# A's fifth row block of x^T phi(k) as seven half-size products of 64 columns, ahead of KV

## The chip, the core and the metric

One core of a Trainium2 chip runs the whole kernel in one launch. The metric is the device time of the execution in microseconds, median of three runs. Every run of the kernel is compared with the kernel before on the same chip. TensorE is called PE (its weight loads PEld), VectorE DVE, ScalarE ACT, GpSimd POOL, SyncE SP.

## The reference

Two blocks of linear attention, A and B, read the same x (1 x 2048 x 640, bf16) with weights of their own, and a gate mixes their outputs row by row.

```python
def _A_ref(x, wqkv, wo):
    B, S, D = x.shape
    H = 32; Dh = D // H
    qkv = (lambda x, *d: x.transpose(*d))((x @ wqkv).reshape(B, S, 3, H, Dh), 2, 0, 3, 1, 4)
    q, k, v = qkv[0], qkv[1], qkv[2]
    phi = lambda t: jnp.where(t > 0, t + 1, jnp.exp(t)) + 1e-6
    pq, pk = phi(q), phi(k)
    kv = jnp.einsum("bhsd,bhse->bhde", pk, v)
    z = jnp.einsum("bhsd->bhd", pk)
    num = jnp.einsum("bhqd,bhde->bhqe", pq, kv)
    den = jnp.einsum("bhqd,bhd->bhq", pq, z)[..., None] + 1e-6
    o = num / den
    return (lambda x, *d: x.transpose(*d))(o, 0, 2, 1, 3).reshape(B, S, D) @ wo
...
g = _sigmoid((x * gate_w).sum(-1, keepdims=True))
return g * a + (1 - g) * b
```

Because v = x Wv, the state of a head is kv = phi(k)^T x Wv. The kernel first forms G = x^T phi(k), a 640 x 640 matrix summed over the 2048 rows of x, then KV = Wv^T G for the 32 diagonal blocks of 20 x 20 (packed six groups wide), then M = KV Wo, and the output is the scaled phi(q) times M.

## The kernel before

x stands in SBUF twice: `xT` with columns on the partitions (five groups of 128, c = 0 to 4), `xn` with rows on them (16 chunks of 128, i = 0 to 15). phi(k) is `pk` (16 chunks of 640 columns), phi(q) transposed is `pqT[b]`. PSUM is used in four slots of two banks; `ps(name, slot)` gives a tile of two banks, `pt[:, 0]` and `pt[:, 1]`, which hold the two halves of 320 columns (HF). Where no slot is named, they take turns.

The stages follow each other on PE: K of A (`k_chunk`), with q of A's first half between, q's second half (`q_pass`), G of A, K of B with A's KV and A's M pushed between the chunks, q of B, G of B, B's KV and M, and the output by pairs of row blocks. From the second K stage on the order of the instructions is the order of the code (`manual_schedule`); the few statements before it, the loads of wv, wo and wk among them, are placed by the scheduler.

G of one block (`g_all`) has two parts. `g_pass` forms row block c = 4 of G, 128 rows, by 16 chunks x 2 halves = 32 matmuls of 320 columns. In its course `z_pass` takes the column sums of phi(k) (`Z`, built by DVE in `z_sum`, `z_half` and `z_last` during q), and DVE turns them into `zsel`. `g_strassen` forms the other 512 rows, seen as a 2 x 2 grid of blocks (256 columns of x, 320 of phi(k), rows of x cut into two halves of 8 chunks), by seven products in the way of Strassen and Winograd, where eight would be needed: 7 x 16 matmuls. The sums of blocks of x are `SX[1]` to `SX[4]` (`x_sum`), those of phi(k) `TK[b][1]` to `TK[b][4]` (`k_sum`); both are DVE adds. The products go into two PSUM tiles, `even` and `odd`, which take turns; p1 (the first product) is copied to SBUF by ACT, u2 and u3 are p1 plus a product, and the results land in `GT[0]` and `GT[1]` (called lo and hi), bf16, one per half of phi(k)'s columns.

Behind the first product stands `rec_pass`: PE forms the denominators for all rows of q from zsel (`by_group`, 40 matmuls on 32 columns of the array each), and `rec(h)` adds the epsilon, multiplies with the gate's factor and takes the reciprocal on DVE, for one half of the rows of q at a time; the result goes to DRAM (`r_store`) and comes back spread over the partitions (`r_load` into `R[h]`). `scale(b, lo, hi, h)` multiplies column groups lo to hi of phi(q), half h, by `R[h]`, on DVE; A's are called between the products of `g_strassen` and after three of B's K chunks.

KV (`kv_mm`) runs over six groups k and, for each, over the five c; a group has two matmuls of 60 or 40 columns on the two halves of the array (`tile_position`). `kv_mask` multiplies with a mask of the diagonal blocks into `KVA`. For A it comes after B's K chunk 1. wv of A is loaded whole (128 x 5 x 640) on SP.

Of the kernel before, what the change touches and what calls it, by code (L numbers as in the profile page):

```python
# [32 lines left out]
def kernel(  # L33
# [273 lines left out]
    def g_pass(b, c, slot):  # L307

        pt = ps(f"g{'AB'[b]}", slot)
        for i in range(ST):  # L310
            if b == 0 and i == 4:
                gate_exp()
            if i == (8 if b else 13):
                zsel = z_pass(b)
                if b:
                    p_diff(part[0])
                else:
                    x_sum(2)
                    gate_done(0)
            if b == 1 and i == 13:  # L320
# [12 lines left out]

    def x_sum(k, cuts=(0, hc)):

        x11, x21 = [xn[:, 0:hc, n:n + ic] for n in (0, ic)]
        x12, x22 = [xn[:, hc:ST, n:n + ic] for n in (0, ic)]
        a, b, op = {
            1: (x21, x22, ALU.subtract), 2: (x11, SX[1], ALU.subtract),
            3: (x21, x11, ALU.subtract), 4: (x12, SX[2], ALU.subtract),  # L340
        }[k]
        for lo, hi in zip(cuts, cuts[1:]):
            add_rows(SX[k][:, lo:hi], a[:, lo:hi], b[:, lo:hi], op)

# [20 lines left out]

    def g_prod(pt, left, right, first, lo=0, hi=hc):

        for i in range(lo, hi):
            for n in range(2):
                nc.tensor.matmul(  # L370
                    pt[:, n, 0:HF], lhsT=left[:, i, n * P:(n + 1) * P], rhs=right[:, i, :],
                    start=(first and i == 0), stop=(i == hc - 1), skip_group_check=not first,
                )

    def g_strassen(b, den):

        x11, x12 = [xn[:, k:k + hc, 0:ic] for k in (0, hc)]
        x22 = xn[:, hc:ST, ic:2 * ic]
# [4 lines left out]
        def temp(name):  # L383
            return work.tile([P, 2, HF], FP32, tag="osb", name=name, bufs=3)

        def add(dst, pt, sb):
            nc.vector.tensor_tensor(out=dst, in0=pt[:, :, 0:HF], in1=sb[:], op=ALU.add)

        even, odd = ps("gs0", 0), ps("gs1", 1)
        g_prod(even, x11, b11, True, 0, 1 - b)  # L390
        rec = den()
        rec(0)
        g_prod(even, x11, b11, True, 1 - b)
        p1 = temp("p1")
        nc.scalar.copy(out=p1[:], in_=even[:, :, 0:HF])
        if b == 0:
            x_sum(3)
        else:
            rec(1)
        g_prod(odd, SX[2], TK[b][2], True)  # L400
        u2 = temp("u2")
        add(u2[:], odd, p1)
        if b == 0:
            x_sum(4)
        else:
            p_diff(part[2])
            p_diff(part[3])
            m_sum(0)
        g_prod(even, x12, b21, False)
        nc.scalar.copy(out=lo[:, 0:2, :], in_=even[:, :, 0:HF])  # L410
        if b == 0:
            rec(1)
        r_load(b, 1, nc.scalar)
        if b == 0:
            wq[1] = load_w(1, "q", nc.scalar)
        scale(b, 0, 2, 0)
        g_prod(odd, SX[3], TK[b][3], False)
        u3 = temp("u3")
        add(u3[:], odd, p1)
        scale(b, 2, 4, 0)  # L420
        even = ps("gs0", 0)
        g_prod(even, SX[1], TK[b][1], True)
        if b == 1:
            load_wo(1, nc.sync)
        add(hi[:, 2:4, :], even, u3)
        scale(*((b, 0, 2, 1) if b else (b, 4, 5, 0)))
        g_prod(odd, x22, TK[b][4], False)
        if b == 1:
            scale(1, 4, 5, 0)
        add(lo[:, 2:4, :], odd, p1)  # L430
        if b == 1:
            scale(1, 2, 4, 1)
        g_prod(even, SX[4], b22, False)
        for n in range(2):
            nc.vector.tensor_tensor(out=hi[:, n, :], in0=even[:, n, 0:HF], in1=u2[:, n], op=ALU.add)
        if b == 0:
            scale(0, 0, 2, 1)
    def z_pass(b):

        dst = ps(f"z{'AB'[b]}", 1 - b)[:, 0, 0:DT * H]  # L440
        for c in range(DT):
            nc.tensor.matmul(
                dst[:, c * H:(c + 1) * H], lhsT=mixed(Z[:, 0], c), rhs=ones[:], start=True, stop=True,
            )
        zsel = work.tile([P, DT, H], BF16, tag="zsel", name="zsel")
        nc.vector.tensor_tensor(
            out=zsel[:], in0=dst.rearrange("p (c h) -> p c h", h=H),
            in1=headE[:, None, :].to_broadcast([P, DT, H]), op=ALU.mult,
        )
        return zsel  # L450
# [16 lines left out]
    def kv_mask(src):  # L467
# [3 lines left out]
        for i, n in ((0, 2), (2, 1)):  # L471
            w = WT[i]
            for r in range(2):
# [4 lines left out]
                )  # L478

    def kv_a():  # L480

        pt = ps("kvA")
        kv_mm(0, pt[:, 0])
        kv_mask(pt[:, 0])

# [30 lines left out]
    def rec_pass(b, zsel, slot):  # L516
# [5 lines left out]
        def rec(h):  # L522
            cols = slice(h * RB, (h + 1) * RB)
            d1 = work.tile([P, RB], FP32, tag="d1", name="d1", bufs=1)
            nc.vector.scalar_tensor_tensor(
                out=d1[:], in0=pt[:, 0, cols], scalar=EPS, in1=ge[b][:, cols], op0=ALU.add, op1=ALU.mult
            )
            rT = work.tile([P, RB], BF16, tag="rT", name="rT")
            with nc.allow_low_precision(reason="a fp32 reciprocal, stored as the bf16 that multiplies bf16"):
                nc.vector.reciprocal(out=rT[:], in_=d1[:])  # L530
            eng = nc.scalar if h else nc.sync
            r_store(b, h, rT, eng)
            if h == 0:
                r_load(b, h, eng)
# [61 lines left out]

    def tmp(name, tag):
        return work.tile([P, HF], FP32, tag=tag, name=name)

    class Pair:  # L600
# [44 lines left out]
        def p6(self):  # L645
            prod(self.at("x"), xT[:, :, 0:SH], TM[1], self.i, True)
            self.u6 = tmp("u6", "ex")
            nc.scalar.copy(out=self.u6[:], in_=self.at("x"))  # L648

        def u25(self):  # L650
            self.v = tmp("v", "zr")
            out_add(self.v[:], self.u6[:], self.p15)

# [22 lines left out]
    def load_w(b, which, eng, cuts=(0, DT)):  # L676
        lo = {"q": 0, "k": D, "v": 2 * D}[which]
        t = wpool.tile([P, DT, D], BF16, tag="w" + which, name=f"w{which}{'AB'[b]}")
# [33 lines left out]

    def g_all(b):

        zsel = g_pass(b, DT - 1, 2 - b)
        g_strassen(b, lambda: rec_pass(b, zsel, 3 - b))

# [4 lines left out]
    for n in range(2):  # L722
        for i in range(CB if n else 0, CB * 2 * n):
            k_chunk(0, i, lifted=i % 2 == 0)
        for m in (0, 2):
# [14 lines left out]
    with tc.manual_schedule():  # L740
        for i in range(hc + 1, ST):
# [26 lines left out]
        q_pass(1, [(m, h) for h in range(2) for m in range(DT)], {0: 2, 2: 3, 4: 4}, (1, 3, 5, 6, 7, 8, 9))  # L768
        g_all(1)
        banks.close()  # L770
# [120 lines left out]
```

## Time and profile before

| | us |
|---|---|
| median of 3 runs (182.39 to 182.6) | 182.46 |
| the profiled execution | 182.69 |
| its span | 180.9 |
| PE busy | 177.1 |
| DVE busy | 147.5 |
| ACT busy | 85.8 |
| POOL busy | 5.4 |

The span runs from the first to the last instruction of the program on the core; the profiled execution's own time lies 1.8 us above it. The clock that PE was granted is 1.0 throughout. Busy time of PE is the time in which at least one matmul is under way, and matmuls overlap, so a full row of PE says that it had no gap, not that it was at its peak. In the timelines a row is a run of equal instructions of one engine: start, length, engine, source line, operation, what it writes and reads, how many, and in brackets the idle time before it with what ended it.

### The profile page before, as it was taken

To read this page: it belongs to the slowest core of one execution; us is meant where nothing else is said; L and a number is where in the kernel's file an instruction comes from. 1 tells how busy PE (TensorE), PEld (TensorE's weight loads), DVE (VectorE), ACT (ScalarE), POOL (GpSimd) and SP (SyncE) were. 2 spreads that over 40 slices of the span, in tenths; PEclk is the share of its full clock that TensorE was granted. 3 is DMA by queue.
4 is the path that set the end of the run, shared out by engine and by line. 5 is a ranking of instruction groups with operands and counts; after the bars stand their busy time and mean duration, and the time that the engine had idled before them with its cause. 6 is when DMAs were issued, how large, how long until landed. Compare 5 with 4: busy or idle time off the path is not lost.

```text
span 180.9 us, 3414 instructions
## 1 busy us (share of the span) xinstructions
PE 177.1 (98%) x1340; PEld 119.3 (66%) x1345; DVE 147.5 (81%) x247; ACT 85.8 (47%) x140; POOL 5.4 (3%) x18
## 2 busy tenths in 40 slices
PE   8999999999999999999999999999999999999993
PEld 4566657765577777777775555677777777677772
DVE  0386868989998896888778999969999799977863
ACT  2245846889971101378784779921101863111010
POOL 6000000000000000000000000000003200000000
PEclk9999999999999999999999999999999999999999
DMA  5999999523100216431116000000325451133323
GB/s 179 209 269 173 244 370 284 112 49 134 58 0 6 70 47 209 110 108 36 57 34 190 19 0 0 0 4 14 125 78 132 137 181 50 36 109 112 109 92 127
DMA packets 22842, 19.33 MB, mean 107 GB/s; under 512 B 10538, under 2 KB 22058, under 8 KB 22826
## 3 DMA queue, kind: packets, MB, share of 16 engines
q1 hardware_dynamic: 20744, 16.95, 34.0%
q10 hardware_dynamic: 2082, 2.17, 3.6%
q8 instruction: 10, 0.16, 0.4%
q14 instruction: 6, 0.05, 0.1%
HBM read 12.29 MB, written 4.53 MB: 93 GB/s over the span
## 4 chain that ended last, share of the span: by engine, by line
PE 97%; issue 0%; DVE 0%
PE gs L370 17%; PE kA L218 12%; PE ox L590 12%; PE kB L218 12%; PE qB L281 12%; PE qA L281 6%; PE oz L590 6%; PE qA L291 5%; PE gB L329 2%; PE gA L329 2%; PE ow L590 2%; PE xt L165 2%; PE qA L301 1%; PE mA L494 1%; PE s L494 1%; PE oy L590 1%
## 5 line engine op out<-in xcount | busy, mean ns | idle before, releaser
L218 PEld LDWEIGHTS <-xT 128*128 128x128 bf16 x320 | 31.0, 98 | 12.8 <-DVE xT L243 0.2
L210 DVE TENSOR_SCALAR e<-e 128x640 bf16<-128x640 bf16 (+2 forms) x53 | 18.9, 357 | 7.3 <-ACT e L205 6.7
L218 PE MATMUL kB<-wkB,xT 128*128 128x320 bf16 x160 | 23.1, 299 | 0.0
L218 PE MATMUL kA<-wkA,xT 128*128 128x320 bf16 (+1 forms) x160 | 22.9, 301 | 0.0
L281 PE MATMUL qB<-xT,wqB 128*128 128x512 bf16 x98 | 21.6, 379 | 0.1
L205 ACT ACTIVATE e<-kB 128x640 bf16<-128x640 f32 x16 | 11.2, 703 | 15.8 <-DMA wqB<-in_B_wqkv_dram 9.4
L281 PEld LDWEIGHTS <-wqB 128*128 128x128 bf16 x100 | 11.7, 117 | 9.7
L205 ACT ACTIVATE e<-kA 128x640 bf16<-128x640 f32 x16 | 11.2, 704 | 8.3 <-PE kA L218 8.3
L205 ACT ACTIVATE e<-qA 128x1024 bf16<-128x1024 f32 (+1 forms) x11 | 10.4, 946 | 6.4 <-PE qA L291 5.1
L648 ACT COPY u<-ox 128x320 f32<-128x320 f32 x8 | 3.4, 425 | 20.6 <-PE ox L590 20.6
L205 ACT ACTIVATE e<-qB 128x1024 bf16<-128x1024 f32 x10 | 10.2, 1023 | 5.6 <-PE qB L281 4.9
L370 PEld LDWEIGHTS <-xn 128*128 128x128 bf16 x96 | 9.2, 98 | 3.9 <-issue 0.4
L370 PEld LDWEIGHTS <-S 128*128 128x128 bf16 x96 | 9.4, 98 | 3.6
L281 PE MATMUL qA<-xT,wqA 128*128 128x512 bf16 x49 | 10.9, 379 | 0.1
L214 DVE SCALAR_TENSOR_TENSOR pk<-kB,e 128x640 bf16<-128x640 f32 x12 | 9.9, 824 | 1.2
L590 PEld LDWEIGHTS <-xT 128*128 128x128 bf16 x85 | 8.1, 98 | 2.9
L590 PEld LDWEIGHTS <-pqTB 128*128 128x128 bf16 x80 | 7.8, 98 | 3.3 <-issue 0.2
L590 PEld LDWEIGHTS <-pqTA 128*128 128x128 bf16 x80 | 7.7, 98 | 2.9
L370 PE MATMUL gs<-pk,xn 128*128 128x320 bf16 x64 | 9.5, 299 | 0.0
L281 PEld LDWEIGHTS <-wqA 128*128 128x128 bf16 x50 | 5.9, 117 | 4.8
L291 PE MATMUL qA<-xT,wqA 128*128 128x512 bf16 x38 | 8.9, 379 | 0.1
L212 DVE TENSOR_TENSOR pk<-pk,e 128x640 bf16<-128x640 bf16 x12 | 5.9, 492 | 2.8 <-ACT pk L209 2.2
(123 smaller groups left out, 296.9 us busy)
## 6 DMA issues: line engine op xcount, KB each, us to landing
xn<-in_A_x_dram SPq DMA_DIRECT2D x1, 2240.0 KB, 10.0
out_dram<-pk SPq DMA_DIRECT2D x14, 160.0 KB, 1.8
wvA<-in_A_wqkv_dram SPq DMA_DIRECT2D x1, 800.0 KB
wkB<-in_B_wqkv_dram SPq DMA_DIRECT2D x1, 800.0 KB, 4.7
wqB<-in_B_wqkv_dram ACTq DMA_DIRECT2D x1, 800.0 KB, 6.5
wvB<-in_B_wqkv_dram SPq DMA_DIRECT2D x1, 800.0 KB
MA<-mA_dram SPq DMA_DIRECT2D x1, 800.0 KB, 6.1
MB<-mB_dram SPq DMA_DIRECT2D x1, 800.0 KB
```

The lines of the kernel that those rows point to most:

```text
L165: nc.tensor.matmul(warm[:, 1, 0:n], lhsT=one_l, rhs=one_r[:, 0:n], start=True, stop=True)
L205: nc.scalar.activation(out=e[:], in_=src, func=ACT.Exp)
L210: nc.vector.tensor_scalar(e[:], e[:], 1.0, EPS, op0=ALU.min, op1=ALU.add)
L212: nc.vector.tensor_tensor(out=dst, in0=dst, in1=e[:], op=ALU.max)
L214: nc.vector.scalar_tensor_tensor(out=dst, in0=src, scalar=1.0 + EPS, in1=e[:], op0=ALU.add, op1=ALU.max)
L218: nc.tensor.matmul(pt[:, hf, 0:w], lhsT=xT[:, c, i * P:(i + 1) * P], rhs=wk[b][:, c, hf * HF:hf * HF + w], start=(c == 0), stop=(c == DT - 1),
L281: nc.tensor.matmul(pt[:, u, :], lhsT=mixed(wq[b][:, c, :], m), rhs=xT[:, c, n * HB:(n + 1) * HB], start=(c == 0), stop=(c == DT - 1),)
L291: nc.tensor.matmul(pt[:, u, :], lhsT=mixed(wq[b][:, c, :], m + u), rhs=xT[:, c, n * HB:(n + 1) * HB], start=(c == 0), stop=(c == DT - 1),)
L329: nc.tensor.matmul(pt[:, hf, 0:HF], lhsT=xn[:, i, c * P:(c + 1) * P], rhs=pk[:, i, hf * HF:(hf + 1) * HF], start=(i == 0), stop=(i == ST - 1),
L370: nc.tensor.matmul(pt[:, n, 0:HF], lhsT=left[:, i, n * P:(n + 1) * P], rhs=right[:, i, :], start=(first and i == 0), stop=(i == hc - 1), s ...
L494: nc.tensor.matmul(dst[:w, 0:HF], lhsT=KVA[:rows, k, 0:w], rhs=wo_sb[b][:rows, k, n * HF:(n + 1) * HF], start=True, stop=True,)
L590: nc.tensor.matmul(dst, lhsT=left[:, c, r0:r0 + P], rhs=right[:, c, :], start=(first and c == 0), stop=(c == DT - 1), skip_group_check=not ...
```

## The change

Row block c = 4 of A's G is no longer formed by `g_pass`; it gets seven products of its own (`g_narrow`), with blocks of x of 64 columns. A product of 64 columns uses half of the array, so `quarter` puts the first four chunks of its sum on one half and the last four on the other; the two partial sums land on the two halves of the partitions. GT gets a sixth slice (slice 4 and slice 5 hold the two 64-column blocks, partial sums on top of each other), and KV adds the partial sums by running over the partitions: `load_narrow` lays the last 128 rows of wv on both halves of the partitions, in two DMAs from POOL's queue, and `kv_step` runs over six slices instead of five. `g_pass` remains for B. The sums of x for the narrow products are `narrow_sums`, into the space of M of A (`SN`).

A's other seven products (`g_a`) come in another order: the first and the third tile are used ahead of the denominators (with `z_pass` after three chunks of the third), then SX2·T2, SX3·T3 and x22·T4 go one after another into one tile, each half (`ns=(n,)`) on its own, with DVE's adds by halves. `rec(1)` moves behind them, and its store and load to SP. All ten scalings of A go one by one behind B's K chunks, more of which take the `lifted` form of phi (ACT writes t + 1, DVE a maximum of two bf16 operands). `k_sum(0, 1)` moves forward to the first stage. KV of A and its mask come ahead of B's first K chunk, part of KV ahead of the last narrow product. In the output stage u6 and v share one tile of the tag `osb`.

```diff
-    GT2 = persist.tile([P, 2 * DT, HF], BF16, name="GT")
-    GT = [GT2[:, n * DT:(n + 1) * DT, :] for n in range(2)]
+    GT2 = persist.tile([P, 2 * (DT + 1), HF], BF16, name="GT")
+    GT = [GT2[:, n * (DT + 1):(n + 1) * (DT + 1), :] for n in range(2)]
...
+    SN = {k: flat(M[0], "p c d -> p (c d)", P // 2, k - 1) for k in (1, 2, 3, 4)}
...
+    def narrow_sums():
+        for k in (1, 2, 3, 4):
+            x_sum(k, f0=2 * ic, w=P // 2, dst=SN)
...
+    def g_a():
...
+        even, third = ps("gs0", 2), ps("gs2", 1)
+        g_prod(even, x11, b11, True)
+        gate_exp()
+        p1 = g_temp("p1")
+        nc.scalar.copy(out=p1[:], in_=even[:, :, 0:HF])
+        g_prod(third, SX[1], t[1], True, 0, 3)
+        zsel = z_pass(0, 3)
+        x_sum(2)
+        gate_done(0)
+        g_prod(third, SX[1], t[1], True, 3)
+        rec = rec_pass(0, zsel, 3)
+        rec(0)
+        x_sum(3)
+        g_prod(even, x12, b21, False)
+        nc.scalar.copy(out=lo[:, 0:2, :], in_=even[:, :, 0:HF])
+        wq[1] = load_w(1, "q", nc.scalar)
+        odd = ps("gs1", 0)
+        for n in range(2):
+            g_prod(odd, SX[2], t[2], True, ns=(n,))
+        u2 = g_temp("u2")
+        halves(u2, odd, p1)
+        x_sum(4, 0, hc // 2)
+        u3 = g_temp("u3")
+        for n in range(2):
+            g_prod(odd, SX[3], t[3], False, ns=(n,))
+            nc.vector.tensor_tensor(out=u3[:, n], in0=odd[:, n, 0:HF], in1=p1[:, n], op=ALU.add)
+            if n == 0:
+                x_sum(4, hc // 2, hc)
+        halves(hi[:, 2:4], third, u3)
+        for n in range(2):
+            g_prod(odd, x22, t[4], False, ns=(n,))
+        halves(lo[:, 2:4], odd, p1)
+        rec(1)
+        for n in range(2):
+            g_prod(third, SX[4], b22, False, ns=(n,))
+        halves(hi[:, 0:2], third, u2)
+        r_load(0, 1, nc.sync)
+        kv = g_narrow()
+        kv_mask(kv)
+
+    def g_narrow():
...
+        def quarter(pt, left, right, first):
+
+            for i in range(hc // 2):
+                for r in range(2):
+                    rows = slice(r * P // 2, (r + 1) * P // 2)
+                    j = r * hc // 2 + i
+                    nc.tensor.matmul(
+                        pt[rows, 0:HF], lhsT=left[:, j, :], rhs=right[:, j, :], start=(first and i == 0),
+                        stop=(i == hc // 2 - 1), tile_position=(0, rows.start), skip_group_check=not first,
+                    )
...
+        pair = ps("gn0", 2)
+        A, B = [pair[:, n, 0:HF] for n in range(2)]
+        quarter(A, x11, b11, True)
+        p = g_temp("pn")
+        p1, p15 = p[:, 0], p[:, 1]
+        nc.scalar.copy(out=p1, in_=A)
+        quarter(B, SN[2], t[2], True)
+        u = g_temp("un")
+        u6, v = u[:, 0], u[:, 1]
+        nc.scalar.copy(out=u6, in_=B)
+        pair = ps("gn1", 0)
+        C, G = [pair[:, n, 0:HF] for n in range(2)]
+        quarter(C, x12, b21, True)
+        add(lo[:, DT - 1, :], C, p1)
+        quarter(A, SN[1], t[1], False)
+        nc.scalar.copy(out=p15, in_=A)
+        quarter(B, SN[3], t[3], False)
+        add(hi[:, DT, :], B, p15)
+        quarter(G, SN[4], b22, True)
+        add(v, u6, p15)
+        add(hi[:, DT - 1, :], G, v)
+        kv = ps("kvA", 1)[:, 0]
+        wide = range(DT - 1)
+        kv_step(kv, (0, 1), wide, True)
+        quarter(B, x22, t[4], False)
+        add(lo[:, DT, :], B, p1)
+        kv_step(kv, (2, 3, 4, 5), wide)
+        kv_step(kv, (0, 1, 2), (DT - 1,))
+        kv_step(kv, (3, 4, 5), (DT - 1, DT))
+        kv_step(kv, (0, 1, 2), (DT,))
+        return kv
...
-            eng = nc.scalar if h else nc.sync
+            eng = nc.scalar if h and b else nc.sync
...
+    def load_narrow():
+
+        src = A_wqkv[2 * ic:D, 2 * D:3 * D].rearrange("(n p) f -> p n f", n=2)
+        for r in range(2):
+            nc.gpsimd.dma_start(out=wv[0][r * P // 2:(r + 1) * P // 2, DT - 1:DT + 1, :], in_=src)
...
-    wv[0] = load_w(0, "v", nc.sync)
+    wv[0] = load_w(0, "v", nc.sync, (0, DT - 1))
+    load_narrow()
...
-                k_sum(0, 1)
+                narrow_sums()
...
-        g_all(0)
+        g_a()
...
+        scales = {1: (0, 0), 2: (1, 0), 3: (2, 0), 4: (3, 0), 5: (4, 0), 7: (0, 1), 9: (1, 1), 10: (2, 1), 11: (3, 1), 13: (4, 1)}
         for i in range(ST):
-            k_chunk(1, i, lifted=i in (5, 7, 9, 13))
-            if i in (3, 5, 7):
-                scale(0, i // 2 + 1, i // 2 + 2, 1)
+            k_chunk(1, i, {0: 0, 1: 2, 2: 1}.get(i), lifted=i in (1, 2, 3, 5, 7, 9, 11, 13))
+            if i in scales:
+                c, h = scales[i]
+                scale(0, c, c + 1, h)
...
             if i == 1:
-                kv_a()
```

In the `g_strassen` that is left (for B), every branch that was for A is gone.

More of the change, by code (lines that the diff above doesn't have):

```diff
@@ L310, in g_pass @@
         for i in range(ST):
[L311 to L320, printed above, removed]
+            if i == 8:
+                zsel = z_pass(b, 0)
+                p_diff(part[0])
+            if i == 13:
                 p_diff(part[1])
@@ L364, in z_last, with g_prod @@
         add_rows(Z[:, 0, 0:HF], Z[:, 0, 0:HF], Z[:, 0, HF:D], ALU.add)
-    def g_prod(pt, left, right, first, lo=0, hi=hc):
+    def g_prod(pt, left, right, first, lo=0, hi=hc, ns=(0, 1)):
         for i in range(lo, hi):
-            for n in range(2):
+            for n in ns:
                 nc.tensor.matmul(
@@ L373, in g_prod, with g_temp, k_blocks @@
                 )
-    def g_strassen(b, den):
-        x11, x12 = [xn[:, k:k + hc, 0:ic] for k in (0, hc)]
-        x22 = xn[:, hc:ST, ic:2 * ic]
+    def g_temp(name):
+        return work.tile([P, 2, HF], FP32, tag="osb", name=name, bufs=3)
+    def k_blocks():
         b11 = pk[:, 0:hc, 0:HF]
         b21, b22 = [pk[:, hc:ST, n * HF:(n + 1) * HF] for n in range(2)]
-        lo, hi = GT
-        def temp(name):
-            return work.tile([P, 2, HF], FP32, tag="osb", name=name, bufs=3)
+        return b11, b21, b22
@@ new lines, in g_a, with halves @@
+    def g_a():
+        x11, x12, _, x22 = x_blocks(0, ic)
+        b11, b21, b22 = k_blocks()
+        t = TK[0]
+        lo, hi = GT
+        def halves(dst, pt, sb):
+            for n in range(2):
+                nc.vector.tensor_tensor(out=dst[:, n], in0=pt[:, n, 0:HF], in1=sb[:, n], op=ALU.add)
+        even, third = ps("gs0", 2), ps("gs2", 1)
[31 more added lines that the diff above has]
+        rec(1)
+        for n in range(2):
+            g_prod(third, SX[4], b22, False, ns=(n,))
[3 more added lines that the diff above has]
+        kv_mask(kv)
@@ new lines, in g_narrow, with add @@
+    def g_narrow():
+        x11, x12, _, x22 = x_blocks(2 * ic, P // 2)
+        b11, b21, b22 = k_blocks()
+        t = TK[0]
+        lo, hi = GT
+        def quarter(pt, left, right, first):
[7 more added lines that the diff above has]
+                    )
+        def add(dst, a, b):
+            nc.vector.tensor_tensor(out=dst, in0=a, in1=b, op=ALU.add)
+        pair = ps("gn0", 2)
[29 more added lines that the diff above has]
+        return kv
@@ new lines, in kv_step @@
+    def kv_step(dst, ks, cs, fresh=False):
+        for k in ks:
+            for c in cs:
+                for p0, hf, d0, w in kv_groups(k):
+                    nc.tensor.matmul(
+                        dst[p0:p0 + w, k * WT[0]:k * WT[0] + w], lhsT=wv[0][:, c, hf * HF + d0:hf * HF + d0 + w],
+                        rhs=GT[hf][:, c, d0:d0 + w], start=(fresh and k == ks[0] and c == cs[0]), stop=(c == cs[-1]),
+                        tile_position=(0, p0), skip_group_check=True,
+                    )
@@ L386, in add, with g_strassen @@
+    def g_strassen(den):
+        x11, x12, _, x22 = x_blocks(0, ic)
+        b11, b21, b22 = k_blocks()
+        lo, hi = GT
+        temp = g_temp
         def add(dst, pt, sb):
@@ L478, in kv_mask @@
                 )
[L480 to L484, printed above, removed]
     def m_rows(k):
@@ L677, in load_w @@
         lo = {"q": 0, "k": D, "v": 2 * D}[which]
-        t = wpool.tile([P, DT, D], BF16, tag="w" + which, name=f"w{which}{'AB'[b]}")
+        t = wpool.tile([P, DT + (which == "v"), D], BF16, tag="w" + which, name=f"w{which}{'AB'[b]}")
         for c0, c1 in zip(cuts, cuts[1:]):
@@ L724 @@
             k_chunk(0, i, lifted=i % 2 == 0)
+        if n:
+            k_sum(0, 1)
         for m in (0, 2):
```

84 lines of the change are left out of this document (33 added, 51 removed).

## The prediction

> **What bounds the kernel now.** I read the page first, for the shares of the engines and of the chain that ended last.
>
> ```profile
> span 180.9 us, 3414 instructions
> ...
> PE 177.1 (98%) x1340; PEld 119.3 (66%) x1345; DVE 147.5 (81%) x247; ACT 85.8 (47%) x140; POOL 5.4 (3%) x18
> ...
> PE 97%; issue 0%; DVE 0%
> ```
>
> PE is busy for 98% of the span and carries 97% of the chain. Time that PE loses in the middle is not made up anywhere; time that another engine loses costs nothing until PE waits for it. The second view is the chain in order of time (start, length, what), cut to the stage that the change rebuilds.
>
> ```profile
> 49.01 3.53 PE gA L329 x26
> 52.54 0.17 PE zA L442 x5
> ...
> 53.81 1.21 PE denA L177 x40
> 55.02 15.05 PE gs L370 x110
> 70.06 2.72 PE kB L218 x20
> 72.78 0.96 PE kvA L462 x60
> 73.75 4.18 PE kB L218 x30
> ```
>
> From the first gA product to the second block of kB nothing but PE stands in the chain: A's 16 row blocks for column group 4 (32 matmuls), seven half-size products gs (112), then B's first two K chunks with A's KV put between them. How it stays gapless is seen in PE's timeline, where a row is a run of equal matmuls.
>
> ```profile
> 48.85 3.69 PE L329 MATMUL gA<-pk,xn 128*128 128x320 bf16 x26
> ...
> 56.86 2.34 PE L370 MATMUL gs<-pqTB,S 128*128 128x320 bf16 x16
> 59.03 2.34 PE L370 MATMUL gs<-pk,xn 128*128 128x320 bf16 x16
> ...
> 67.73 2.34 PE L370 MATMUL gs<-pk,MB 128*128 128x320 bf16 x16
> ```
>
> Of the gs rows, the 16 matmuls that start at 56.86 are SX2·T2 into the tile called odd; the 16 at 59.03 go to the other tile, even. While they run, DVE adds odd to p1 (the row of 0.82 us in DVE's timeline below); only then does the next product into odd begin. One matmul of this shape lasts 299 ns and sixteen last 2.34 us, so they start (2.34 - 0.30) / 15 = 0.136 us apart.
>
> ```profile
> 50.47 1.71 DVE L546 TENSOR_TENSOR GT<-GT 128x1280 bf16<-128x1280 bf16 x3
> ...
> 53.23 0.32 DVE L446 TENSOR_TENSOR zsel<-zA,headE 128x160 bf16<-128x160 f32 x1
> ...
> 59.30 0.82 DVE L387 TENSOR_TENSOR u<-gs,p 128x640 f32<-128x640 f32 x1 [0.89 <-PE gs L370]
> ...
> 70.10 0.89 DVE L435 TENSOR_TENSOR GT<-gs,u 128x320 bf16<-128x320 f32 x2 [1.35 <-PE gs L370]
> ```
>
> **The change part by part, in PE's order.** Three facts of the built order, with each instruction's waits, carry the sum. It has 2764 rows on PE against 2692: 32 matmuls fewer of gA, 56 more of 64 columns, 12 more in KV. The rows that matter, shortened, with their number on the engine:
>
> ```
> PE  601 Ldweights GT [waits PE, DVE]              z_pass
> PE  776 Matmult gs<-pqTB,S  [waits DVE]           first half of SX3.T3
> PE  792 Matmult gs<-pqTB,S  [waits DVE]           second half of SX3.T3
> PE  808 Matmult gs<-pqTB,xn [waits DVE]           first half of x22.T4
> DVE  81 TensorTensor u<-gs,p [waits PE, ACT]      u2, first half
> DVE  82 TensorTensor u<-gs,p                      u2, second half: no wait
> DVE  84, 86 TensorTensor u<-gs,p [waits PE]       u3, each half
> PE  888, 920, 936 Matmult gn<-pqTB,MA [waits ACT] narrow products 2, 4, 5
> ```
>
> *PE's own work.* Out: 32 x 0.136 = 4.35 us. In: 56 matmuls of 64 columns. They issue in pairs on the two halves of the array. The nearest rows with such pairs are KV and, with four tiles of 32 columns, denA.
>
> ```profile
> 53.74 1.27 PE L177 MATMUL denA<-pqTA,zsel 128*32 128x256 bf16 x40
> ...
> 72.71 1.03 PE L462 MATMUL kvA<-GT,wvA 128*60 128x60 bf16 x60
> L462 PEld LDWEIGHTS <-wvA 128*60 128x60 bf16 x40 | 0.8, 109 | 0.3 <-issue 0.3
> ```
>
> Forty denA matmuls in 1.27 us are ten groups of four: with 0.28 us for the last one's own length, nine steps of 0.11 us, about what one 256-column matmul takes alone. So tiles run together, and a pair of 320 columns costs one step of 0.136: 28 x 0.136 = 3.81 us, with no overlap 56 x 0.136 = 7.62. I take 3.81, by those two rows. KV grows from 60 to 72 matmuls: 12 x 0.96 / 60 = 0.19. Entry into and exit from tiled mode come twice before and twice after. Net -0.35 us.
>
> The Trainium skill (TensorEngine Tiling (Array Packing), Restrictions and Gotchas) says that column tiling switches Fast Weight Load off, which speaks against splitting a product into twice as many loads. The KV row shows it harmless here: a load lasts 109 ns, yet 60 of them pass in 0.96 us; were two loads in line for each pair, 28 x (0.218 - 0.136) = 2.3 us would be added.
>
> *z_pass asks earlier.* It stood behind 26 gA matmuls and now stands behind 16 + 6. PE reaches it at 48.85 + 22 x 0.136 = 51.84, counted from the start of the first gA matmul. Its weights are the sums Z, which DVE finishes at 50.47 + 1.71 = 52.18; DVE is in an unbroken row from 40 us on and gets no less work there. Stall 52.18 + 0.05 - 51.84 = 0.39. Behind it on PE stands everything else; zsel on DVE is not delayed, since it runs at 53.23 after a phi step.
>
> *Three products in a row into one tile.* Before, odd and even took turns. Now SX2·T2, SX3·T3 and x22·T4 go into odd one after another, in halves, with half-size adds between. The halves share one tile, and the waits are on the tile: the first u2 add waits for PE and the second does not, so the first one waits for both halves; PE 776 then waits for DVE. PE idles from its normal next start to the end of both adds: 299 - 136 ns of the last matmul, 0.03 for DVE to start (the adds of 70.10 behind matmuls that end at 67.73 + 2.34 = 70.07), 0.89 for two adds, 0.03 back: 1.11 us. For u3 each half has its own wait: PE 792 waits for the add of half one and PE 808 for that of half two, though they write other columns: twice 0.163 + 0.03 + 0.49 + 0.03 = 0.71, together 1.42. The add's length is the group row
>
> ```profile
> L435 DVE TENSOR_TENSOR GT<-gs,u 128x320 bf16<-128x320 f32 x4 | 1.8, 486 | 1.3 <-PE gs L370 1.3
> L648 ACT COPY u<-ox 128x320 f32<-128x320 f32 x8 | 3.4, 425 | 20.6 <-PE ox L590 20.6
> ```
>
> In between, DVE has half of x_sum(4), which fits into the wait. SX4·b22 goes into third, whose adds are done by then.
>
> *The narrow block.* Products 1 and 2 lie in one tile (pair gn0), and so do C and G (gn1). PE 888, product 2, waits for ACT's copy of product 1: 0.163 + 0.03 + 0.425 + 0.03 = 0.65. Product 3 (C) goes straight on for 4 x 0.136 = 0.54, so product 4, which waits for the copy of 2, stalls 0.65 - 0.54 = 0.11. Product 5 waits for the copy of 4: 0.65. G and the last one find their readers done, since a quarter or a KV step lies between. The last KV step waits for the last add (0.16 + 0.03 + 0.49 after the product, against 25 KV pairs of 0.03 = 0.75): 0 to 0.15, I take 0.05. Together 1.46 us. rec(1), 2.2 us of DVE, stands ahead of the adds of hi 0 and 1; they end before KV's third step asks for them.
>
> *The start.* load_narrow issues two DMAs from POOL's queue, 64 x 2 x 640 bf16 = 0.16 MB each, behind the memset of headE, so from 2.64 us on.
>
> ```profile
> 2.52 0.12 POOL L151 MEMSET headE<- 128x32 bf16 x1
> 2.50:3.50 1.00, 1.00 (x4) 0.29 (x2) 0.00 (x0) 0.78 (x1) 0.90 (x6) 1.00 1.05 365
> 3.50:4.50 1.00, 1.00 (x11) 0.92 (x10) 0.16 (x1) 0.51 (x1) 0.00 (x0) 1.00 1.07 321
> ...
> 4.86 0.80 PE L218 MATMUL kA<-wkA,xT 128*128 128x320 bf16 x3
> ...
> 5.70 5.38 PE L218 MATMUL kA<-wkA,xT 128*128 128x320 bf16 x37
> ```
>
> The DMA engines are full then (share 1.05, 365 GB/s), with wkA, which PE is waiting for: 40 kA matmuls would need 40 x 0.136 + 0.16 = 5.6 us and take from 4.86 to 11.08, 6.2. The added 0.33 MB at 321 GB/s is 1.0 us if all of it goes ahead of wkA, and nothing if all of it comes behind. A part of it will be in time to hinder: I take 0.3. The trace has no DMA from POOL, so neither end is excluded.
>
> The Trainium skill (DMA: Bandwidth & Descriptors, Issuing engines are not separate DMA queues) has all queues on the same 16 engines, interleaved, and gives about 1 us to the first byte on POOL's path. By that the first load would be moving by 3.6 us, in the thick of wkA, and this term could be 0.5 or more.
>
> *What costs nothing.* Ten scalings of one column group move behind B's K chunks. In this stretch (the columns are length, then busy time of PE, its loads, DVE and ACT)
>
> ```profile
> 70.00:94.50 24.50, 24.50 (x234) 18.04 (x233) 20.24 (x40) 16.65 (x25) 0.00 (x0) 1.00 0.27 82
> 74.73 1.34 DVE L475 TENSOR_TENSOR KVA<-kvA,maskE 60x240 bf16<-60x240 f32 x4
> ...
> 78.51 0.68 DVE L579 TENSOR_TENSOR pqTA<-pqTA,R 128x1024 bf16<-128x1024 bf16 x1
> ```
>
> DVE has 4.3 us idle. It gets seven more scalings (7 x 0.68 = 4.8) and loses one of double width, the mask of 1.34 and the last two adds of 0.89, all of which now come earlier, and four chunks turn to the lifted form, in which ACT, with 7.9 us idle, does a further pass for DVE. The PSUM tiles of the first chunks are free by then. If that cover were gone, each late scaling would cost its 0.68. narrow_sums takes the place of the moved k_sum(0, 1) (four adds of 512 against one of 2560 columns); r_store and r_load of half 1 go to SP, wqB no longer waits behind them on ACT, and wvB on SP, now behind r_load, is wanted only by B's own KV, a whole stage later.
>
> **The sum.** -0.35 + 0.39 + 1.11 + 1.42 + 1.46 + 0.3 = +4.33 us. The profiled execution took 182.69 us (span 180.9 and 1.8 around it), so 187.0 in its frame; the median of the three runs is 182.46, 0.23 lower, which gives 186.8.
>
> **The rivals.**
> - *Releases at half a tile* (the faster side). If a half's add held only its own columns, every add and copy (0.49 and 0.43) would fit under the 1.09 us of the other half or the 0.54 us of another product, and the stalls of 1.11, 1.42 and 1.41 would vanish. It decides at one point: whether PE's next half starts before the add on the other half has ended. For it: the adds are half-size instructions of their own, so each could be released alone. Against: the waits on PE 776, 792 and 888. Time: 182.46 - 0.35 = 182.1 with Z in time and the load behind wkA; each of these two, where it fails, takes that gain back (0.39, 0.3).
> - *The start decides more.* All of the narrow load ahead of wkA: +1.0 in place of 0.3, 187.5. For it: full DMA engines and PE waiting. Against: POOL's descriptors may come late, behind wkA, when PE has its weights.
> - *Pairs don't overlap.* +3.8 us: 190.6. Against: denA and kvA.
>
> **How the numbers follow.** The forecast, waits as the built order has them, with a light start, has 0.85, time 186.8; the heavy start 0.08; half-tile releases 0.05; no overlap 0.02. The bounds of the unknown costs are 0 to 1.0 for the start, that is -0.3 and +0.7, and some 0.4 either way on the stalls' ten hand-overs between engines at 0.03 each way, each of which may be twice that or nothing: 186.1 to 187.9; the low end is set at 185.9, towards the half-tile case. A change under 0.2% (0.36 us) can't be told from none. Only half-tile releases could come below that: faster 0.03, within 0.2% 0.02, slower 0.95.
>
> **What would show it.** In the changed profile PE should be idle about 1.1 us once and 0.7 us twice in the gs products, released by DVE's adds, and 0.65 us twice in gn, released by ACT's copies; z_pass should wait 0.4 us for DVE's GT sums. kB should start near 74 us instead of 69.9 and everything after it be shifted by the same amount. Right but mis-sized at the start: first qA matmul well after 11.08 - 0.16 = 10.9 us. Wrong altogether: gs products without gaps in PE's timeline.

## The result, and the profile after

The changed kernel takes 189.29 us (median of 7 runs, 189.03 to 192.95), the kernel before 182.51 beside it. The ratio is 1.038, with a 95% interval of 1.035 to 1.040: slower by 6.8 us where +4.3 was forecast. Slower was right; the time lies 1.4 us above the range.

The first profile of the changed kernel fell in an execution of 192.94 us that was disturbed, mostly at the start; the profile read below is of the same kernel taken once more (188.95 us), and the first one is quoted only where it says so.

Page of the changed kernel: the span, busy time of the engines, and the larger of the two DMA queues named instruction, which carries engine code (packets, MB, share).

```profile
span 187.2 us, 3516 instructions
...
PE 178.1 (95%) x1381; PEld 119.6 (64%) x1381; DVE 149.9 (80%) x264; ACT 88.9 (47%) x145; POOL 6.7 (4%) x20
...
q8 instruction: 11, 0.18, 0.4%
```

The span grew by 6.3 us, from 180.9, and PE's busy time by 1.0. So PE now stands still for 9.1 us, 5.3 more than before. PE's timeline of the changed kernel (start, length, what, and in brackets the idle time before) shows where, from the start to the output stage (a row at the edge of a view ends with it: more kB follow the 27 at 76.38, and more qB the 4 at 99.77):

```profile
7.93 3.98 PE L219 MATMUL kA<-wkA,xT 128*128 128x320 bf16 x28 [0.80 <-DMA wkA<-in_A_wqkv_dram]
11.74 4.48 PE L292 MATMUL qA<-xT,wqA 128*128 128x512 bf16 x20
...
51.85 0.98 PE L371 MATMUL gs<-pqTB,S 128*128 128x320 bf16 x6
53.07 0.37 PE L548 MATMUL zA<-ones,GT 128*128 128x32 bf16 x5 [0.24 <-DVE GT L646]
...
58.13 2.34 PE L371 MATMUL gs<-pqTB,S 128*128 128x320 bf16 x16
61.51 1.25 PE L371 MATMUL gs<-pqTB,S 128*128 128x320 bf16 x8 [1.05 <-DVE u L394]
63.34 1.25 PE L371 MATMUL gs<-pqTB,S 128*128 128x320 bf16 x8 [0.58 <-DVE u L421]
65.17 2.33 PE L371 MATMUL gs<-pqTB,xn 128*128 128x320 bf16 x16 [0.58 <-DVE u L421]
67.34 2.34 PE L371 MATMUL gs<-pk,MB 128*128 128x320 bf16 x16
69.61 0.73 PE L449 MATMUL gn<-pk,xn 128*64 128x320 bf16 x8
70.86 0.73 PE L449 MATMUL gn<-pqTB,MA 128*64 128x320 bf16 x8 [0.52 <-ACT pn L462]
71.40 0.74 PE L449 MATMUL gn<-pk,xn 128*64 128x320 bf16 x8
72.15 0.73 PE L449 MATMUL gn<-pqTB,MA 128*64 128x320 bf16 x8
73.40 0.73 PE L449 MATMUL gn<-pqTB,MA 128*64 128x320 bf16 x8 [0.51 <-ACT pn L472]
...
74.48 0.43 PE L494 MATMUL kvA<-GT,wvA 128*60 128x60 bf16 x16
74.79 0.73 PE L449 MATMUL gn<-pqTB,xn 128*64 128x320 bf16 x8
75.33 1.11 PE L494 MATMUL kvA<-GT,wvA 128*40 128x40 bf16 x56
76.38 3.84 PE L219 MATMUL kB<-wkB,xT 128*128 128x320 bf16 x27
...
99.77 1.03 PE L282 MATMUL qB<-xT,wqB 128*128 128x512 bf16 x4
...
156.70 1.52 PE L690 MATMUL ow<-MB,pqTB 128*128 128x320 bf16 x10 [0.55 <-DMA MB<-mB_dram]
```

Every stall of the forecast is there, released by the engine that it named: DVE's sums for z_pass, DVE's u once at 1.05 and twice at 0.58, ACT's copies twice. A stall costs more than the idle time in brackets, because the last matmul overlaps the next one that would have followed: behind SX2·T2's sixteen the next start would be 58.13 + 16 x 0.136 = 60.31, and SX3·T3 starts at 61.51, 1.20 later.

Two things at the edges of this list were not in the sum or were small in it. The first qA starts at 11.74 instead of 10.91. And in the output stage the first use of M of B (ow) waits for the load of it, which it did not before. (kB starts at 76.38, not near 74 as forecast: A's KV, 0.97 us, now lies ahead of it, so by the prediction's own sum 69.90 + 0.97 + 4.33 = 75.2 was due.) PE's timeline of the kernel before has these rows for the same two places of the second half:

```profile
94.36 0.81 PE L281 MATMUL qB<-xT,wqB 128*128 128x512 bf16 x2
...
150.58 1.52 PE L590 MATMUL ow<-MB,pqTB 128*128 128x320 bf16 x10
```

Cut at the first qA, at the first qB and at ow, the two spans compare so (us):

| stretch | before | changed | more |
|---|---|---|---|
| to the first qA | 10.91 | 11.74 | 0.83 |
| first qA to first qB | 83.45 | 88.03 | 4.58 |
| first qB to ow | 56.22 | 56.93 | 0.71 |
| ow to the end | 30.32 | 30.50 | 0.18 |
| span | 180.9 | 187.2 | 6.3 |

The forecast had 0.3, 4.03, 0 and 0 for these. The same cuts serve for every experiment below.

### The profile page after: what moved, and what is told of

It reads as the page before. It is cut to its first block, busy times and chain, and to the rows that moved or that the text cites. A ratio compares the mean times of both kernels' runs of the same rounds, so it can differ in the third digit from the quotient of the medians.

```text
span 191.2 us, 3511 instructions
## 1 busy us (share of the span) xinstructions
PE 180.0 (94%) x1376; PEld 120.6 (63%) x1381; DVE 150.1 (78%) x264; ACT 88.9 (46%) x145; POOL 6.7 (3%) x20
## 4 chain that ended last, share of the span: by engine, by line
PE 81%; DMA 8%; DVE 6%; ACT 2%; issue 1%; SPq 0%; DVEq 0%
PE gs L371 15%; PE kB L219 11%; PE qB L282 11%; PE kA L219 11%; PE ox L690 10%; PE qA L292 4%; DMA xT<-in_A_x_dram 4%; PE oz L690 3%; PE gn L449 2%; PE gB L324 2%; PE qA L282 2%; DMA MB<-mB_dram 2%; PE ow L690 2%; DVE GT L646 2%; DVE pqTA L213 1%; DMA xn<-in_A_x_dram 1%
## 5 line engine op out<-in xcount | busy, mean ns | idle before, releaser
L219 PEld LDWEIGHTS <-xT 128*128 128x128 bf16 x320 | 31.5, 100 | 16.6 <-DMA xT<-in_A_x_dram 2.3
L219 PE MATMUL kA<-wkA,xT 128*128 128x320 bf16 (+1 forms) x160 | 24.7, 314 | 2.6 <-DMA xT<-in_A_x_dram 2.0
L213 DVE TENSOR_TENSOR pk<-pk,e 128x640 bf16<-128x640 bf16 x16 | 7.9, 493 | 2.8 <-ACT pk L210 1.6
L690 PEld LDWEIGHTS <-xT 128*128 128x128 bf16 x85 | 8.1, 98 | 2.9
L371 PE MATMUL gs<-pqTB,S 128*128 128x320 bf16 x48 | 7.3, 299 | 1.6 <-DVE u L394 1.0
```

Source lines behind the costliest of these rows:

```text
L213: nc.vector.tensor_tensor(out=dst, in0=dst, in1=e[:], op=ALU.max)
L219: nc.tensor.matmul(pt[:, hf, 0:w], lhsT=xT[:, c, i * P:(i + 1) * P], rhs=wk[b][:, c, hf * HF:hf * HF + w], start=(c == 0), stop=(c == DT - 1),
L371: nc.tensor.matmul(pt[:, n, 0:HF], lhsT=left[:, i, n * P:(n + 1) * P], rhs=right[:, i, :], start=(first and i == 0), stop=(i == hc - 1), s ...
L690: nc.tensor.matmul(dst, lhsT=left[:, c, r0:r0 + P], rhs=right[:, c, :], start=(first and c == 0), stop=(c == DT - 1), skip_group_check=not ...
```

## The experiments

**The changed kernel once more.** No edit; it gave the profile above.

> The changed kernel once more, unaltered, for a profile in an execution without disturbance. If the longer waits in its output stage (3.5 us for the store of B's M) belong to the execution that was profiled, its span is near 187.4 us and they are gone; if they belong to the change, it is near 191. Both theories of the start expect the first qA matmul later than 10.91 us: by about 1.8 us if the narrow load holds up xT's transposes, by 1.0 at most if only its bytes count.

188.95 us, span 187.2. The stores of M of B land in 2.9 us instead of the 3.5 of the first profile, and ow waits 0.55 instead of 1.20: smaller, but not gone. At the start it is wkA that PE waits for, as the prediction had named it. In the first profile PE had waited there for xT, for 2.02 us.

**The narrow loads on SP.**

```diff
-            nc.gpsimd.dma_start(out=wv[0][r * P // 2:(r + 1) * P // 2, DT - 1:DT + 1, :], in_=src)
+            nc.sync.dma_start(out=wv[0][r * P // 2:(r + 1) * P // 2, DT - 1:DT + 1, :], in_=src)
```

> The changed kernel with the two narrow loads of wv issued by SP, behind wv, instead of by POOL. Theory: loads from POOL's queue, in flight from 4 us on, make xT's transposes land late, which costs some 1.8 us at the start; without them the first qA matmul is back at 10.9 us, all waits in G stay as they are, and the time is before + 4.6 = 187.1 us. Rival, the start is late because of 0.33 MB more to move: the bytes are the same, the first qA stays late, and the time stays at 188.8 to 189.3.

188.24 us (188.01 to 189.0), ratio 1.031 (1.028 to 1.035). PE's timeline:

```profile
10.65 4.48 PE L292 MATMUL qA<-xT,wqA 128*128 128x512 bf16 x20
...
98.69 0.81 PE L282 MATMUL qB<-xT,wqB 128*128 128x512 bf16 x3
...
155.72 1.52 PE L690 MATMUL ow<-MB,pqTB 128*128 128x320 bf16 x10 [0.65 <-DMA MB<-mB_dram]
```

The start is back (10.65), with the same bytes in the kernel; so the late start came from the loads being in flight early. The middle is unchanged, 88.04. But 187.1 was missed by 1.1: from the first qB to ow it takes 57.03 and to the end 30.58, together 1.07 more than before. A loss behind the first qB, where the diff changes only two temporaries, was now a finding to explain.

**Before, with the two loads on POOL, and on ACT.** To the kernel before, these lines are added behind the first loads; the second kernel has `nc.scalar` for `nc.gpsimd`.

```diff
+    src = A_wqkv[4 * P:D, 2 * D:3 * D].rearrange("(n p) f -> p n f", n=2)
+    for r in range(2):
+        nc.gpsimd.dma_start(out=M[0][r * P // 2:(r + 1) * P // 2, 0:2, :], in_=src)
```

> The kernel before plus the two narrow loads from POOL's queue, into a part of M of A that nothing reads before it is overwritten; nothing else is changed. Theory (xT's transposes held up): +1.8 us, 184.3, xT lands 2 to 3 us later and PE waits about 2 us in the kA group for it. Rival, the prediction's term (only bytes ahead of wkA count): +0.3, at most +1.0, 182.8 to 183.5.

> The kernel before plus the two narrow loads as in the run with POOL's queue, but issued on ACT's queue behind its pieces of wkA. Theory (what costs is the stretch in which they share the DMA engines with wkA, not POOL's path as such): as with POOL, first qA at 11.4 to 11.9 instead of 10.9, 183.2 to 183.7. Rival (POOL's own path, with its larger packets, is what hinders): no more than 0.2 us, 182.5 to 182.8.

On POOL 183.72 us (median of 10, 183.61 to 186.92) against 182.56, ratio 1.008 (1.005 to 1.011); on ACT 184.43 against 182.71, ratio 1.010 (1.008 to 1.012). The start in PE's timeline, first with POOL, then with ACT:

```profile
6.71 5.18 PE L218 MATMUL kA<-wkA,xT 128*128 128x320 bf16 x36 [0.48 <-DMA wkA<-in_A_wqkv_dram]
11.72 4.48 PE L291 MATMUL qA<-xT,wqA 128*128 128x512 bf16 x20
```

```profile
9.29 2.90 PE L218 MATMUL kA<-wkA,xT 128*128 128x320 bf16 x20 [0.92 <-DMA xT<-in_A_x_dram]
12.03 4.48 PE L291 MATMUL qA<-xT,wqA 128*128 128x512 bf16 x19
```

The loads alone cost 0.81 at the first qA on POOL's queue, as in the changed kernel, and 1.12 on ACT's. Neither the 1.8 nor the 0.3 of the two theories was met: 0.81 lies within the rival's bound of 1.0, and the time 0.2 us above its 183.5. With ACT's queue both the first qA and the time came out beyond what was expected. POOL's own path is not what hinders, since ACT's queue costs no less. What counts is that 0.33 MB are in flight while wkA and xT are. Which of these two is starved varies with the execution, and with it the cost. So a single profile tells the size only roughly: in the eight profiles without early loads (before and with the loads on SP) the first qA stands anywhere from 10.65 to 11.29. The medians (+1.16 us with POOL, +1.72 with ACT) are the better measure that the loads cost about 1 us or more.

**The halves of odd in tiles of their own.** The loads are on SP; both denominators are read early (`den`), so that slot 3 is free.

```diff
-        odd = ps("gs1", 0)
-        for n in range(2):
-            g_prod(odd, SX[2], t[2], True, ns=(n,))
+        pair = ps("gs1", 0), ps("gs3", 3)
+        odd = [pair[n][:, n:n + 1] for n in range(2)]
...
+        for n in range(2):
+            g_half(odd[n], SX[2], t[2], True, n)
+            add_half(u2[:, n], odd[n], p1[:, n])
```

> The kernel with the loads on SP, and the two halves of odd in PSUM tiles of their own (slots 0 and 3), each half-size add behind its own half; both denominators are read early, so that their slot is free. Theory (waits are on tiles, not on columns): the waits of 1.05, 0.58 and 0.58 us in the gs products are gone, and the time falls by 2.2 to 2.6 us against the run with the loads on SP, to about 184.6. Rival (a half-size product with a half-size add is too short to hide DVE's answer in any tile): the waits stay, no change, 187.1.

185.72 us (185.31 to 185.96), ratio 1.016 (1.013 to 1.018): 2.5 us less than with the loads alone on SP. From the first qA to the first qB it takes 85.35 us, against 88.04.

```profile
57.69 4.51 PE L379 MATMUL gs<-pqTB,S 128*128 128x320 bf16 x32
62.03 2.34 PE L379 MATMUL gs<-pqTB,xn 128*128 128x320 bf16 x16
64.21 2.34 PE L371 MATMUL gs<-pk,MB 128*128 128x320 bf16 x16
```

Same products, same halves, same adds, no gap: 48 matmuls from 57.69 to 64.21 are 0.136 each. So the waits were on the tile, and the adds are not too long for the cover. The Trainium skill (Perfetto Trace Analysis, Matmuls) lets matmul groups rotate through PSUM banks so that the readers of one overlap the next; here the halves lay in banks of their own before too, and it was the tile that had to differ.

**The narrow products in tiles of their own.** As in the last experiment, and besides products 1 and 2 in slots 2 and 0, C and G in slot 3; B's first K chunks change slots with it.

```diff
-        pair = ps("gn0", 2)
-        A, B = [pair[:, n, 0:HF] for n in range(2)]
+        A, B = [ps(f"gn{n}", 2 - 2 * n)[:, 0, 0:HF] for n in range(2)]
...
-        pair = ps("gn1", 0)
+        pair = ps("gn2", 3)
```

> The run with the halves of odd in tiles of their own, and besides the narrow products 1 and 2 in tiles of their own (slots 2 and 0), C and G in the third slot. Theory (waits are on tiles): the waits of 0.71, 0.21 and 0.71 us in the narrow block, counted from the normal next start, are gone, -1.6 us against that run, 184.1. Rival (half-width products are too short to hide ACT's copies): the waits stay, 185.7.

184.02 us (12 runs, 183.36 to 184.97), ratio 1.006 (1.004 to 1.009), so 1.0 percentage points or 1.7 us less than the last kernel; from the first qA to the first qB 83.72 us, 1.63 less.

```profile
66.42 0.73 PE L461 MATMUL gn<-pk,xn 128*64 128x320 bf16 x8
66.99 0.71 PE L461 MATMUL gn<-pqTB,MA 128*64 128x320 bf16 x8
67.53 0.71 PE L461 MATMUL gn<-pk,xn 128*64 128x320 bf16 x8
```

The products follow each other at 0.54 to 0.57 us. So the prediction's rival, releases at half a tile, had the lengths right: adds and copies of 0.49 and 0.43 do fit under the other half. Only this kernel's tiles did not allow it.

**The code packets among the stores.** The page gives 10 code packets of 0.16 MB for before and 11 of 0.18 MB for the changed kernel, against 2685 and 2762 recorded matmuls and weight loads: one of 16 KB for about each 250 instructions of PE. M of B goes to DRAM in six stores, and comes back in one load. The stretch that holds the stores (46.5 to 51.1 us after the first qB) has this in the view of the DMA queues, first before, then the changed kernel (the queue's packets, MB and share; then the store's issues, KB and median time to landing):

```profile
q1 hardware_dynamic: 728, 0.82, 60.3%
...
mB_dram<-pk SPq DMA_DIRECT2D x4, 150.0 KB, 2.1
```

```profile
q8 instruction: 1, 0.02, 1.6%
...
mB_dram<-pk SPq DMA_DIRECT2D x4, 150.0 KB, 2.9
```

In the changed kernel a code packet lies in the stretch; 1.6% of 16 engines over 4.6 us is 1.2 us of one engine. The stores take 2.9 us to land instead of 2.1. To tell a cause from company, PE's stream was lengthened by 38 instructions (19 matmuls and their weight loads) with the columns in sum unchanged, once in the changed kernel with the loads on SP and once in the kernel before:

```diff
-    for n in (HB,) * 6 + (HB // 2,):
+    for n in (HB // 4,) * 26:
         nc.tensor.matmul(warm[:, 1, 0:n], lhsT=one_l, rhs=one_r[:, 0:n], start=True, stop=True)
```

> The changed kernel with the loads on SP; the only edit is that the seven warm-up matmuls at the very start are cut into 26 of 128 columns, which puts 38 instructions more into PE's stream and no work. Theory: PE's code arrives as 16 KB packets, one for about each 250 of PE's instructions, and in the changed kernel one of them falls among the stores of M of B and delays the load of it by 0.4 us; 38 instructions earlier it falls ahead of the stores, the packet is at 45.5 to 46 us after the start of B's q (48.5 without the edit), M of B is used 0.3 to 0.45 us earlier, 187.8. Rival (the stores are slow for another reason, of the changed order or tiles): no change, 188.2.

> The kernel before with the same cut of the warm-up matmuls into 26, nothing else. Theory: here the code packet came behind the stores of M of B (51.3 us after the start of B's q); 38 instructions earlier it falls among them (48.5 to 49), the stores land later, M of B is used 0.3 to 0.45 us later, 182.9. Rival: no change, 182.5.

The changed kernel fell to 187.74 us, ratio 1.028 (1.023 to 1.033) against 1.031 without the edit; the intervals overlap, and the profile has to decide. The kernel before rose to 183.59 against 182.81, ratio 1.005 (1.002 to 1.007). The queues in the same stretch of the changed kernel, where the code queue has no row any more, and its rows in PE's timeline:

```profile
q1 hardware_dynamic: 730, 0.82, 60.1%
...
mB_dram<-pk SPq DMA_DIRECT2D x4, 150.0 KB, 2.0
```

```profile
98.78 0.81 PE L282 MATMUL qB<-xT,wqB 128*128 128x512 bf16 x3
...
155.06 1.52 PE L690 MATMUL ow<-MB,pqTB 128*128 128x320 bf16 x10
```

The same two views of the kernel before, where the code queue has a row now:

```profile
q8 instruction: 1, 0.02, 1.6%
...
mB_dram<-pk SPq DMA_DIRECT2D x4, 150.0 KB, 3.0
```

```profile
94.37 0.81 PE L281 MATMUL qB<-xT,wqB 128*128 128x512 bf16 x3
...
151.65 1.52 PE L590 MATMUL ow<-MB,pqTB 128*128 128x320 bf16 x10 [0.90 <-DMA MB<-mB_dram]
```

The same edit takes the packet out of the stretch in one kernel and puts it in in the other. From the first qB to ow it is now 56.28 (57.03 without the edit) and 57.28 (56.22): -0.75 and +1.06, both more than the 0.3 to 0.45 expected, and of these four profiles only those with the packet among the stores have ow waiting for M of B. All the kernels of this document bear it out. In the same stretch, six (the changed kernel, with the loads on SP, both with tiles of their own, with u6 and v apart, and the kernel before with the cut warm-up) have the packet: the stores of 150 KB land in 2.9 to 3.1 us, and first qB to ow takes 56.93 to 57.29. Five (before, before with the loads on POOL or on ACT, the changed kernel with the cut warm-up, and all at once) have none: 2.0 to 2.1 us where a landing time is given, and 56.22 to 56.51.

**u6 and v apart.** In the changed kernel with the loads on SP:

```diff
-            u = g_temp("u")
-            self.u6, self.v = u[:, 0], u[:, 1]
+            u, v = [work.tile([P, HF], FP32, tag=t, name=t, bufs=n) for t, n in (("u6", 1), ("v", 2))]
+            self.u6, self.v = u[:], v[:]
```

> The changed kernel with the loads on SP, and u6 and v of the output stage in tiles of their own again. Theory: sharing one tile gives ACT's copy of u6 a further wait, by which PE's product that follows it starts 0.02 to 0.06 us late, some 0.23 us over seven pairs; with tiles of their own these are gone, -0.25, 188.0. Rival (the waits come from elsewhere): no change.

188.05 us (187.94 to 188.31), ratio 1.027 (1.023 to 1.032). The runs alone do not tell 0.2 us; the rows do. A late pair of PE's products in the kernel with one tile, then with two:

```profile
179.69 0.84 PE L690 MATMUL ox<-TM,pqTB 128*128 128x320 bf16 x5
180.41 0.84 PE L690 MATMUL ox<-TM,D 128*128 128x320 bf16 x5
```

```profile
155.95 1.52 PE L690 MATMUL ow<-MB,pqTB 128*128 128x320 bf16 x10 [0.57 <-DMA MB<-mB_dram]
...
179.75 0.84 PE L690 MATMUL ox<-TM,pqTB 128*128 128x320 bf16 x5
180.43 0.84 PE L690 MATMUL ox<-TM,D 128*128 128x320 bf16 x5
```

Five matmuls need 0.68 us. With one tile the second product of the pair starts 0.72 after the one ahead of it, 0.04 late; with two it is 0.68. From ow to the end (the span is 186.3) it is 30.35, against 30.58 with one tile and 30.32 before: 0.23 of the 0.26 lost there.

**All of it at once.** Loads on SP, tiles of their own in both places, z_pass after four chunks of third instead of three (`g_prod(third, SX[1], t[1], True, 0, 4)`), the warm-up in 26, and u6 and v apart (u6 in a tile of the ring `osb`, to fit).

> The changed kernel with everything that cost time mended at once: loads on SP, the halves of odd and the narrow products in tiles of their own, z_pass after four chunks of third instead of three, the warm-up in 26 matmuls, u6 and v apart. Theory: what is left of the change is its own account on PE, seven narrow products of 0.54 us each and 0.38 us more in KV and mode changes against the 4.35 us of gA taken out, about -0.2, with about 0.1 us of waiting left over and M of B some 0.1 us earlier: within 0.3 us of before, 182.2 to 182.6. Rival, another cost of the change has not been found: above 183.

182.99 us (12 runs, 182.53 to 183.5) against 182.71, ratio 1.0012 (0.9995 to 1.0029): not told from the kernel before, and not better. The expected 182.2 to 182.6 was missed, the "within 0.3 us of before" was met.

```profile
11.12 4.48 PE L292 MATMUL qA<-xT,wqA 128*128 128x512 bf16 x19
...
52.44 0.37 PE L559 MATMUL zA<-ones,GT 128*128 128x32 bf16 x5
...
69.30 0.41 PE L505 MATMUL kvA<-GT,wvA 128*60 128x60 bf16 x16
...
70.12 1.12 PE L505 MATMUL kvA<-GT,wvA 128*40 128x40 bf16 x56
...
94.57 0.81 PE L282 MATMUL qB<-xT,wqB 128*128 128x512 bf16 x2
```

From the first qA to the first qB it takes 83.45 us, what it took before, where 0.2 less was expected. Seven narrow products for gA save 0.57 us (4.35 - 3.78). KV takes 0.36 of it back: its pieces run from 69.30 to 69.58 and from 70.12 to 71.17, 1.33 us against 0.97. z_pass takes 0.17: eight matmuls from 51.22 on would let it start at 52.31, it starts at 52.44, and its five matmuls take 0.22 instead of 0.18. With nearly all waits gone, the narrow block saves nothing.

## Why the prediction missed

Term by term, the forecast and what the rows of the changed kernel give:

| term | forecast | measured |
|---|---|---|
| gA's 32 matmuls out | -4.35 | -4.35 (from the rows before) |
| seven narrow products | 3.81 | 7 x 0.54 = 3.78 |
| KV of 72 | 0.19 | 0.39 |
| z_pass | 0.39 | 0.40 late, 0.04 longer |
| u2 | 1.11 | 1.20 |
| u3, twice | 1.42 | 1.48 |
| narrow block's waits | 1.46 | 0.71 + 0.21 + 0.71 = 1.63 |
| start | 0.3 | 0.83 |
| behind the first qB | 0 | 0.89 |
| sum | 4.33 | 6.29, the spans differ by 6.3 |

- *The step that failed* is the one that ended the sum at B's K: the prediction said that everything after kB would be "shifted by the same amount", and priced what lies behind the first qB at nothing. Two losses arose there, 0.89 us together here and 1.07 with the loads on SP. One was in the diff and not priced: "u6 and v share one tile" stood in the description of the change, and the same reasoning by tiles that found the stalls in G would have found it. The other and larger, a code packet among the stores, could not be seen in the diff; the order's row count (2764 against 2692) was read only as work on PE. This step alone does not make the whole miss: without the 0.89 the time would still be about 0.5 us above the range. The start (0.53 more) and the stalls (0.33 more) stayed within the bounds that the prediction gave them; KV (0.20 more) and the distance of the median had none.
- *The start* was the right mechanism (wkA late behind the narrow load) with the size too small: 0.83 against 0.3, nearer to the heavy start's 1.0, which was given a chance of 0.08. "A part of it will be in time to hinder" was a choice without a row. The sentence drawn from the Trainium skill (DMA: Bandwidth & Descriptors, Issuing engines are not separate DMA queues) asked for 0.5 or more, and the trace agrees with it in size: 0.81 in the kernel before with nothing but the loads. It does not agree in time: the first load is issued at 2.58 us, but POOL's queue has no packet from 2.6 to 5.0 us, where one was expected by 3.6, and 47 of its 96 from 5.0 to 6.0. So that the size fits is luck as far as the 3.6 us go.
- *The stalls in G* came where the built order's waits put them. Two experiments with other tiles removed six of the seven; the one of z_pass shrank from 0.40 to 0.13 us with one more chunk ahead of it. Each was 0.01 to 0.10 longer than worked out, 0.38 us over seven stalls, less the 0.05 taken for KV's last step, which did not come. The hand-overs between engines, taken at 0.03 each way, were too short: at u2 DVE starts 0.10 behind the end of the last matmul and PE 0.05 behind the end of the adds.
- *KV* costs 0.39 more, not 0.19: its two pieces, 74.48 to 74.79 and 75.33 to 76.38, are 1.36 us for 72 matmuls, 0.019 each, against 0.97 / 60 = 0.016 before in one piece. Why each takes longer is not shown.
- *Pairs overlap*, as argued from denA and kvA: 28 pairs in 3.78 us. So the rival of 190.6 falls, though the measured time lies nearer to it than to the forecast.
- The median is some 0.5 us further from the median before than the two profiled executions are from each other. The start differs from execution to execution, and the runs scatter (183.61 to 185.79 in nine of the ten with the loads alone); that the one explains the other is not shown.

What stays open is why KV's matmuls take 0.019 us each, and why a code packet of 1.2 us on one engine makes stores of 150 KB land 0.8 to 1.0 us later. The kernel with everything mended takes 86.83 us from the first qB to the end, against 86.54 before; the kernel before with the loads on POOL or on ACT takes 86.73 with the same code there, so up to 0.2 of these 0.29 us may be a difference between executions.

## What to carry to other kernels

Read a wait by the tile it is on: two halves that are written and read apart still wait for each other if they share a tile, and the same edit with tiles of their own was worth 4.2 us here. Price every line of a change with the same question, the temporaries in far stages too, and do not load early what is needed late while the engine is waiting for its first weights. Before splitting a product to save an eighth of it, add up what must stay exposed around it: here the saving was 0.57 us, and KV's further matmuls and z_pass had taken it back even with nearly all waits gone.

## What the runs showed of the hardware

Code arrives in 16 KB packets during the execution, one for about 250 PE instructions, and such a packet among six stores makes them land 0.8 to 1.0 us later. So 38 instructions more at the start, with no more work, made the kernel before 0.8 us slower in the runs, and the changed one 0.75 faster in the second half of its profile (0.5 in the runs, within their scatter), by what happened 140 us later. A comparison of two kernels with different numbers of instructions holds such shifts, in either direction, and a difference of about a microsecond or less should be looked up in the queues before it is put down to the edit.
